# The last group's half results: evacuated by two engines, and stored from ScalarE's queue instead of SyncE's

**Chip and metric.** One core of one Trainium2 chip. The metric is the device time of one launch in microseconds (us), on the slowest (here the only) core.

## The reference

Two spectral layers and two dense layers in turn, on x of 2048 x 1024 in bf16:

```python
def _A_ref(x, w_r, w_i):                       # spectral layer
    X = rfft2(x.astype(float32)) * (w_r + 1j * w_i)
    return irfft2(X, s=(S, D)).astype(bfloat16)

def _B_ref(x, w1, b1, w2):                     # dense layer, F = 3584
    h = einsum("bsd,df->bsf", x, w1) + b1
    return einsum("bsf,fd->bsd", h * tanh(softplus(h)), w2)

for A, B in (two times the same weights):
    x = x + _A_ref(_layernorm(x), w_r, w_i)
    x = x + _B_ref(_layernorm(x), w1, b1, w2)
```

## The kernel before

The FFTs are matrix products. A spectral layer handles its frequencies in eight groups g. Step `i2` of a group gives two half results in PSUM, the memory that TensorE writes to. They are copied ("evacuated") into the tile `U` in SBUF, the on-chip memory of the tiles, in bf16. The last step, `i4`, needs `U` with other rows on the partitions, so each group is stored into DRAM (`u_scratch`) and read back transposed into `UT`. Groups 0 to 6 are stored whole; group 7, the last, is stored in two halves so that the first can leave early.

```python
def i2(g, half):
    ...                                        # matmuls into ps (lines 738 and 756)
    dst = u.ap[:, 8 * half:8 * half + 8, :].rearrange("p a b -> p (a b)")
    if g > 4 or (half == 0 and g % 2 and li):
        self.op(dve, lambda e: e.tensor_copy(dst, ps), reads=banks, parts=[u.res])            # line 764
    else:
        self.op(act, lambda e: e.activation(dst, ps, ACT.Copy), reads=banks, parts=[u.res])   # line 766

def u_turn(g, half):
    u = U[g % 3]
    if g == 7:
        h = slice(8 * half, 8 * half + 8)
        if half == 0:
            self.r_ud[g].begin()
        self.dma(sp, self.u_d[g][:, h, :], u.ap[:, h, :], f"uwh{half}", reads=[u.res], parts=[self.r_ud[g]])
    elif half:
        self.dma(sp, self.u_d[g], u.ap, f"uw{g % 3}", reads=[u.res], writes=[self.r_ud[g]])
    if g and (half == 0) == (g == 7):
        u_back(g - 1)                          # for g = 7: read-back of 6 BETWEEN the two stores
    if g == 7 and half:
        u_back(7)

def u_back(g):                                 # 16 rows x 128 x 256 bytes
    for i, prog in enumerate((sp, act) if g == 7 else (sp,)):
        l = slice(64 * i, 64 * i + 64) if g == 7 else slice(0, P)
        self.dma(prog, self.UT.ap[g:P:8, l, :], self.u_d[g][l].rearrange("l r n -> r l n"), ...,
                 reads=[self.r_ud[g]], parts=[self.UT.res])

def i4(self, lo, nb, u0, n, bank, staged=None):
    ...                                        # matmuls, line 875
    self.group(fns, reads=[self.UT.res, self.r_mt], writes=rb)    # waits for ALL of UT
    ...                                        # VectorE adds into x, line 881
```

Each engine takes its program in order: below, in evac_only, a store whose data is ready at 633.96 us is issued at 637.50, behind an older command. All DMAs (copies between DRAM and SBUF) are issued by the helper line 247, and "SPq" and "ACTq" are the sequencers of SyncE and ScalarE.

Of the kernel before, what the change touches and what calls it, by code (L numbers as in the profile page):

```python
# [179 lines left out]
class KB:  # L180
# [439 lines left out]
    def layer_A(self, li):  # L620
# [7 lines left out]
        dve, act, sp, pool = self.dve, self.act, self.sp, self.pool  # L628
# [97 lines left out]
        def i2(g, half):  # L726

            ps, banks, _ = self.pair()
            v, u = V[g % 2], U[g % 3]
            fns = []  # L730
            mov = lambda c, part: v.ap[:, 2 * c + part, :, :].rearrange("p a b -> p (a b)")

            def cls(kd, re, im):
                t = kd * 3 * P
                for dst, stats in ((re, (0, 2)), (im, (1, 0))):
                    for part in range(2):
                        c = t + stats[part] * P
                        fns.append(lambda e, dst=dst, part=part, c=c: e.matmul(  # L738
                            dst, BD[:, c:c + P], mov(kd, part), start=(part == 0), stop=(part == 1)))
            if half == 0:  # L740
                cls(0, ps[:, 0:256], ps[:, 256:512])
                cls(1, ps[:, 512:768], ps[:, 768:1024])
            else:
                cls(2, ps[:, 0:256], ps[:, 512:768])

                t = 9 * P
                if g == 0:
                    outs = [[(i, part, (0, 2)[part]) for part in range(2)] for i in range(2)]
                else:
                    outs = [[(0, 0, 0), (0, 1, 2), (1, 0, 0), (1, 1, 2)], [(0, 0, 1), (0, 1, 0), (1, 0, 2), (1, 1, 3)]]  # L750
                for m, terms in enumerate(outs):
                    for n, (i, part, tab) in enumerate(terms):
                        for kd in range(2):
                            rows = slice(64 * kd, 64 * kd + 64)
                            dst = ps[:, 512 * kd + 256 + m * P:512 * kd + 256 + (m + 1) * P]
                            fns.append(lambda e, dst=dst, rows=rows, i=i, part=part, tab=tab, n=n, last=len(terms) - 1: e.matmul(
                                dst, BD[rows, t + tab * P:t + (tab + 1) * P], v.ap[rows, 6 + part, i, :],
                                start=(n == 0), stop=(n == last)))
            self.group(fns, reads=[v.res, self.r_bd], writes=banks)
            if half == 0:  # L760
                u.res.begin()
            dst = u.ap[:, 8 * half:8 * half + 8, :].rearrange("p a b -> p (a b)")
            if g > 4 or (half == 0 and g % 2 and li):
                self.op(dve, lambda e: e.tensor_copy(dst, ps), reads=banks, parts=[u.res])  # L764
            else:
                self.op(act, lambda e: e.activation(dst, ps, ACT.Copy), reads=banks, parts=[u.res])  # L766
# [5 lines that stand above are left out]
                h = slice(8 * half, 8 * half + 8)  # L772
                if half == 0:
                    self.r_ud[g].begin()
                self.dma(sp, self.u_d[g][:, h, :], u.ap[:, h, :], f"uwh{half}", reads=[u.res], parts=[self.r_ud[g]])
            elif half:
                self.dma(sp, self.u_d[g], u.ap, f"uw{g % 3}", reads=[u.res], writes=[self.r_ud[g]])
            if g and (half == 0) == (g == 7):
                u_back(g - 1)
            if g == 7 and half:  # L780
                u_back(7)

        def u_back(g):
            for i, prog in enumerate((sp, act) if g == 7 else (sp,)):
                l = slice(64 * i, 64 * i + 64) if g == 7 else slice(0, P)
                self.dma(prog, self.UT.ap[g:P:8, l, :], self.u_d[g][l].rearrange("l r n -> r l n"), f"u{prog.name}{g % 3}",
                         reads=[self.r_ud[g]], parts=[self.UT.res])
# [10 lines left out]
        for step in range(8 + 3):  # L798
            g2, g3, g4, g5 = step, step - 1, step - 2, step - 3
            for h in range(2):  # L800
                if 0 <= g2 < 8:
                    s2(g2, h)
                if 0 <= g2 < 8 and h == 0 and li == 0:
                    filter_bins(g2)
                if 0 <= g3 < 8:
                    s3(g3, h)
                if 0 <= g4 < 8:
                    i1(g4, h)
                if 0 <= g5 < 8:
                    i2(g5, h)  # L810
                    u_turn(g5, h)
            if 0 <= g3 < 8 and g3 + 2 < 8:
                load_tabs(g3 + 2)
            if li == 0 and g2 + 2 < 8:
                load_w(g2 + 2)
            if li == 0 and 1 <= g2 < 9:
                self.keep_filter(g2 - 1)
            if li and 1 <= g2 < 5:
                load_w(g2 + 3)
            if 0 <= g4 < 8 and g4 + 2 < 8:  # L820
                load_btabs(g4 + 2)
# [275 lines left out]
```

## Time and profile before

| | before |
|---|---|
| time, 3 runs | 1071.35 us median (1070.46 to 1071.45) |
| span of the profiled run | 1068.5 us |
| TensorE busy | 973.0 us, 91% |
| TensorE's idle before line 875, for the read-backs | 27.9 us, in two waits |

The kernel is bound by TensorE. What is left to win in the spectral layers' ends is the time in which TensorE waits for `UT`; the prediction below reads that from the chain of waits, the timeline and the DMA view. One thing to know for reading them: a DMA issue's duration is the time that its *issuing engine* spends on it, not the transfer (the store of group 6 takes 0.57 us of issue and lands after 4.33 us). The transfer's end is shown as "landing", or as a DMA piece of the chain.

### The profile page before, as it was taken

The page shows a single profiled execution, that of the slowest core. Times are in us where ns is not written, and L with a number is a line of the kernel's source. Part 1 is how long each engine was busy: PE and PEld are TensorE (multiplying, and loading weights), DVE is VectorE, ACT ScalarE, POOL GpSimd, SP SyncE. Part 2 cuts the span into 40 slices and gives each one's busy share as a digit, 9 for nine tenths or more (in the row PEclk, how much of TensorE's full clock was granted, in tenths as well). Part 3 has the DMA queues.
Part 4 walks back from the last instruction along what each step waited for, and adds up shares of the span by engine and source line. Part 5 has one row for each costly group of instructions (what it writes and reads, how often), then busy time and mean ns, then how long its engine had stood idle before and what let it go on. Part 6 is the DMA issues. An engine that isn't in the chain of part 4 may idle for free. (4 is left out here: it accounts for less than half of the span.)

```text
span 1068.5 us, 14145 instructions
## 1 busy us (share of the span) xinstructions
PE 973.0 (91%) x6089; PEld 509.6 (48%) x6089; DVE 362.4 (34%) x811; ACT 330.2 (31%) x466; POOL 55.3 (5%) x86
## 2 busy tenths in 40 slices
PE   0799479999999999999969965999999999999998
PEld 0677345444444444444427744444444444444443
DVE  7887482600444200033436866451011110000111
ACT  6898253342000234300007843434300013431000
POOL 2042000000000000001310200000000000000000
PEclk9699769999999999999988985999999999999999
DMA  9678732444000122211720885144500002210000
GB/s 293 148 247 252 186 111 85 153 150 126 20 20 21 57 68 73 79 60 38 142 47 30 229 200 139 55 143 146 169 22 20 21 34 70 74 40 11 20 20 29
DMA packets 138958, 102.80 MB, mean 96 GB/s; under 512 B 59952, under 2 KB 117552, under 8 KB 138896
## 3 DMA queue, kind: packets, MB, share of 16 engines
q1 hardware_dynamic: 128528, 78.34, 25.1%
q0 software_dynamic: 7856, 22.94, 7.6%
q10 hardware_dynamic: 2512, 0.62, 0.3%
q8 instruction: 48, 0.79, 0.3%
q14 instruction: 14, 0.11, 0.0%
HBM read 80.85 MB, written 20.71 MB: 95 GB/s over the span
## 5 line engine op out<-in xcount | busy, mean ns | idle before, releaser
L930 PE MATMUL PS<-ARENA 128*128 128x512 bf16 x1792 | 393.7, 382 | 1.6 <-DVE ARENA L917 1.6
L948 PE MATMUL PS<-ARENA 128*128 128x512 bf16 x1792 | 390.0, 379 | 0.0
L934 ACT ACTIVATE ARENA<-PS,B 128x512 bf16<-128x512 f32 x224 | 153.8, 687 | 440.0 <-PE PS L930 440.0
L930 PEld LDWEIGHTS PS<-ARENA 128*128 128x128 bf16 x1792 | 175.5, 98 | 214.3 <-issue 6.0
L948 PEld LDWEIGHTS PS<-ARENA 128*128 128x128 bf16 x1792 | 174.5, 98 | 207.8
L953 DVE TENSOR_TENSOR XS<-PS,XS 128x512 bf16<-128x512 f32 x64 | 44.3, 691 | 566.1 <-PE PS L948 566.1
L436 DVE BATCH_NORM_STATS2 BN<-XS 128x6 f32<-128x512 bf16 x108 | 69.5, 673 | 7.5 <-DMA XS<-in_A_x_dram 6.3
L875 PE MATMUL PS<-MT,ARENA 128*128 128x32 bf16 (+1 forms) x768 | 24.7, 189 | 36.1 <-DMA ARENA<-u_scratch 27.9
L881 DVE TENSOR_TENSOR XS<-PS,XS 128x512 bf16<-128x512 f32 (+1 forms) x40 | 29.1, 789 | 75.8 <-PE PS L875 75.8
L575 ACT ACTIVATE ARENA<-PS 128x1024 bf16<-128x1024 f32 x16 | 16.1, 1018 | 110.8 <-PE PS L569 110.6
L875 PEld LDWEIGHTS PS<-MT,ARENA 128*128 128x128 bf16 x768 | 23.0, 101 | 39.5 <-issue 31.4
L417 ACT ACTIVATE ARENA<-XS 128x1024 bf16<-128x1024 bf16 x20 | 21.1, 1056 | 54.6 <-DVE XS L881 43.6
L695 ACT ACTIVATE ARENA<-PS 128x1024 bf16<-128x1024 f32 x32 | 33.0, 1032 | 9.0 <-PE PS L691 9.0
L650 PE MATMUL PS<-FD,ARENA 128*128 128x256 bf16 (+1 forms) x312 | 33.5, 257 | 2.4 <-DVE ARENA L577 2.4
L724 ACT ACTIVATE ARENA<-PS 128x1024 bf16<-128x1024 f32 x32 | 33.0, 1032 | 3.7 <-PE PS L717 3.7
L717 PE MATMUL PS<-ARENA 128*128 128x256 bf16 x256 | 33.2, 273 | 0.1
L699 DVE TENSOR_TENSOR ARENA<-ARENA 128x1024 bf16<-128x1024 bf16 x32 | 22.1, 690 | 28.1 <-ACT ARENA L695 22.7
L650 PEld LDWEIGHTS PS<-FD,ARENA 128*128 128x128 bf16 x312 | 26.3, 99 | 7.2 <-DVE ARENA L577 2.8
L717 PEld LDWEIGHTS PS<-ARENA 128*128 128x128 bf16 x256 | 24.6, 98 | 9.7 <-DVE ARENA L706 0.9
L912 PE MATMUL PS<-IDENT,ARENA 128*128 128x128 bf16 x256 | 21.6, 242 | 8.3 <-DVE ARENA L479 5.8
L738 PE MATMUL PS<-ARENA,BD 128*128 128x256 bf16 x192 | 25.9, 273 | 0.4 <-DVE ARENA L764 0.2
L912 PEld LDWEIGHTS PS<-IDENT,ARENA 128*128 128x128 bf16 x256 | 18.6, 109 | 14.0 <-DVE ARENA L479 6.9
(66 smaller groups left out, 517.8 us busy)
## 6 DMA issues: line engine op xcount, KB each, us to landing
ARENA<-in_B_w_dram SPq DMA_DIRECT2D x56, 512.0 KB, 4.0
ARENA<-in_B_w_dram SPq DMA_DIRECT2D x56, 256.0 KB, 4.4
u_scratch<-ARENA SPq DMA_DIRECT2D x14, 512.0 KB, 4.1
ARENA<-u_scratch SPq DMA_DIRECT2D x14, 512.0 KB, 5.3
XS<-in_A_x_dram SPq DMA_DIRECT2D x4, 1024.0 KB, 8.6
ARENA<-in_A_x_dram SPq DMA_DIRECT2D x32, 128.0 KB, 3.3
w_scratch<-ARENA POOLq DMA_DIRECT2D x8, 512.0 KB, 5.0
ARENA<-w_scratch POOLq DMA_DIRECT2D x8, 512.0 KB, 3.6
```

The source lines that it names most:

```text
L436: self.op(self.dve, lambda e: e.bn_stats(self.BN[:, j, 6 * h:6 * h + 6], self.XS[:, j, 512 * h:512 * h + 512]), reads=[self.r_xs[j]], part ...
L650: fns.append(lambda e: e.matmul(dst, at(r), FD[:, t:t + dst.shape[-1] * 2], start=start, stop=stop))
L695: self.op(act, lambda e: e.activation(x.ap.rearrange("p a b -> p (a b)"), ps, ACT.Copy, scale=SIG), reads=banks, writes=[x.res])
L717: fns.append(lambda e, c=c, part=part: e.matmul(ps[:, c * 256:(c + 1) * 256], yk.ap[:, part, c * P:(c + 1) * P], t[:, (128, 0)[part]:(384, ...
L724: self.op(act, lambda e: e.activation(v.ap[:, :, i, :], src, ACT.Copy), reads=banks, parts=[v.res])
L875: fns.append(lambda e, l=l: e.matmul(ps[:, w * l:w * l + w], self.UT.ap[:, u0 + l, :], self.MT[:, 8 * lo:8 * lo + w], start=True, stop=True))
L881: self.op(self.dve, lambda e: e.tensor_tensor(xs, src, xs, ALU.add), reads=rb, parts=self.r_xs[lo:lo + nb])
L912: fns.append(lambda e, db=db: e.transpose(PSb[:, bank, db * P:(db + 1) * P], xn.ap[:, db * P:(db + 1) * P], self.IDENT[:]))
L930: fns.append(lambda e, db=db, bank=bank, fl=fl: e.matmul(PS[:, bank, :], wb.ap[:, db, fl * P:(fl + 1) * P], x.ap[:, db, :], start=(db == 0 ...
L934: self.op(act, lambda e, bank=bank, ft=ft: e.activation(at.ap[:, ft, :], PS[:, bank, :], ACT.Mish, bias=self.B1[:, ft:ft + 1]), reads=[sel ...
L948: fns.append(lambda e, i=i, ft=ft: e.matmul(PS[:, bank, :], at.ap[:, ft, t * P:(t + 1) * P], W2[ft].ap[:, h * 512:(h + 1) * 512], start=(i ...
L953: self.op(dve, lambda e: e.tensor_tensor(xs, PS[:, bank, :], xs, ALU.add), reads=[self.r_bank[bank]], writes=[self.r_xs[j]])
```

## The change

Intent: let the last two half results be evacuated by VectorE and ScalarE side by side, and let their stores be issued by ScalarE, which is idle there, so that they don't queue behind SyncE's work.

```diff
-            if g > 4 or (half == 0 and g % 2 and li):
+            if (g > 4 and (g < 7 or half == 0)) or (half == 0 and g % 2 and li):
                 self.op(dve, ... tensor_copy ...)
             else:
                 self.op(act, ... activation Copy ...)
...
-                self.dma(sp, self.u_d[g][:, h, :], u.ap[:, h, :], f"uwh{half}", ...)
+                self.dma(act, self.u_d[g][:, h, :], u.ap[:, h, :], f"uwh{half}", ...)
```

More of the change, by code (lines that the diff above doesn't have):

```diff
@@ L774, in u_turn @@
                     self.r_ud[g].begin()
-                self.dma(sp, self.u_d[g][:, h, :], u.ap[:, h, :], f"uwh{half}", reads=[u.res], parts=[self.r_ud[g]])
+                self.dma(act, self.u_d[g][:, h, :], u.ap[:, h, :], f"uwh{half}", reads=[u.res], parts=[self.r_ud[g]])
             elif half:
```

## The prediction

> **What bounds the kernel now.** I read the page first, then the chain of waits in order of time, the timeline around the end of a spectral layer, the wait table of the DMA queue's own engine, and the DMA view in short windows. The whole kernel is bound by TensorE (973.0 of 1068.5 us busy), so a change elsewhere counts only where TensorE stands still. In section 5 of the page that is the first stage after the spectral block:
>
> ```profile
> L875 PE MATMUL PS<-MT,ARENA 128*128 128x32 bf16 (+1 forms) x768 | 24.7, 189 | 36.1 <-DMA ARENA<-u_scratch 27.9
> ```
>
> TensorE is idle for 36.1 us before this line, 27.9 of them for the bounce of U through DRAM, in two places (once a layer), 14 us each. The change can touch only these two holes. The chain of waits of the second one (start us, us, what):
>
> ```profile
> 630.11 1.24 DVE ARENA L764
> 631.36 4.33 DMA u_scratch<-ARENA
> 635.71 0.54 SPq L247
> 636.29 5.05 DMA u_scratch<-ARENA
> 641.42 4.36 DMA ARENA<-u_scratch
> 645.92 1.03 PE PS L875 x32
> ```
>
> The timeline tells which transfers these are (start us, us in issue; a DMA's line is always the helper's):
>
> ```profile
> 630.11 3.49 DVE L764 CAST ARENA<-PS 128x1024 bf16<-128x1024 f32 x3
> 631.36 0.57 SPq L247 DMA_DIRECT2D u_scratch<-ARENA  x1
> 632.03 0.54 SPq L247 DMA_DIRECT2D ARENA<-u_scratch  x1
> 632.62 2.77 SPq L247 DMA_DIRECT2D u_scratch<-ARENA  x1
> 635.71 0.54 SPq L247 DMA_DIRECT2D ARENA<-u_scratch  x1
> 636.29 1.99 SPq L247 DMA_DIRECT2D u_scratch<-ARENA  x1
> 641.41 0.54 SPq L247 DMA_DIRECT2D ARENA<-u_scratch  x1
> 641.42 0.61 ACTq L247 DMA_DIRECT2D ARENA<-u_scratch  x1
> ```
>
> By the order of the source these are: store of group 6, read-back of 5, store of group 7's first half, read-back of 6, store of 7's second half, read-back of 7 by two queues. The second half of group 7 is in SBUF at 633.60 (three casts from 630.11, 1.21 each), yet its store is issued at 636.29: SyncE's queue first spends 2.77 us issuing the first half's store, then waits until 635.71 for group 6's store to land, then issues that read-back. So 2.7 us go to the order of SyncE's queue.
>
> But the DMA engines are not idle meanwhile. The DMA view from 628 to 648 us, 0.5 us a slice:
>
> ```profile
> DMA  0006997999999999999999999200039998000027
> GB/s 16 0 0 262 385 262 151 267 289 288 264 273 418 341 285 288 231 229 282 330 289 284 223 244 303 102 0 0 0 93 279 267 273 135 2 0 0 16 59 227
> ```
>
> They are full from about 630 to 640.6, empty to 642.8 (the round trip from the last store to the first packet of the last read-back), and full again to 645.0. The only hole to be closed is 2.2 us; the bytes stay the same. In the first layer the same rows run from 114 to 131 us with a hole of 2.2 us from 125.9 to 128.1.
>
> **What the Trainium skill says.** (1) "DMA: Bandwidth & Descriptors", "Issuing engines are not separate DMA queues": transfers from any engine run on the same 16 DMA engines and interleave; a second issuing engine "will only save the time on the sequencer". So no bandwidth is to be expected, only issue order, and this case's wait is just such a case of issue order. (2) The same page, "Queues, rings and completion order": SyncE and ScalarE each own a row of rings on the same engines, "not a DMA engine or descriptor generator of their own", and an engine round-robins between rows. The trace agrees with the first half: the two halves of the last read-back are issued 0.01 us apart, but from 643.2 to 643.6 us SyncE's queue moves 440 packets and ScalarE's 7, and from 644.0 to 644.4 it is 11 and 435. One command is served after the other, they do not alternate. (3) "PSUM — Partial Sum Buffer", "Engine vs sequencer instructions": ScalarE's queue is strict FIFO. A DMA issue that waits on ScalarE therefore holds up the evacuation behind it; the trace before has no such place. (4) "TensorE: Matmul & The Clock Gate", "What's actually happening": after an idle window of about 3.4 us the clock halves and a free-running window decides when it returns. The trace agrees on the fall: the granted clock is 0.50 from 636 us and until 651. A hole of 12 instead of 14 us still falls that low, so no clock is gained; the phase of its return may move by a microsecond or so.
>
> **The change part by part.** *Evacuation of the last half.* Before: DVE, 1.21 us, ends 633.60. After: ScalarE, 1.03 us (same shape, line 766: 1023 to 1165 ns, median 1032). But the first half's store now stands ahead of it in ScalarE's queue and waits for DVE's cast of that half, which ends at 632.44 (630.11 + 1.24, then 1.21 started at 631.23). With an issue of 0.61 us (the issue that ScalarE has here) the activation starts at 633.1 and ends at 634.1. Using two engines thus gains nothing: it is 0.5 us later than DVE was, because ScalarE first waits for DVE. ScalarE itself is idle from 629.9 to 641.4, and VectorE loses a cast that nobody waits behind; neither matters.
>
> *First store.* SyncE no longer stands 2.77 us in its issue, but gains nothing either: its next command, the read-back of 6, waits for group 6's store to land at 635.7 as before.
>
> *Second store.* If ScalarE's issues go through without being held, it is issued at 634.1 + 0.05, or 2.1 us earlier than 636.29, and, more to the point, ahead of the read-back of 6 (635.71, 512 KB in 256-byte packets, some 2 us of packets). In the order of commands it now follows the first half directly. Its landing: first half at 638.6 as before (632.62 + 6.0), plus 256 KB at the measured 280 GB/s, 0.9 us: 639.5, against 641.34. The read-back of 6 is pushed behind by that much, but still ends with the full stretch at 640.6.
>
> *Last read-back.* Issued at 639.5; 1.35 us later its first packet (641.41 to 642.75 before) at 640.9; 2.2 us of packets to 643.1; landing 0.75 after the last packet as before (645.0 to 645.78): 643.8. Against 645.78 that is **2.0 us**. If the stores overtake more of the backlog, by the round robin of the two rows, the hole closes wholly: 2.2, and with some better packing at most 2.7. It cannot be much more, since the same 2.6 MB or so stand ahead of the end either way.
>
> *Downstream.* The matmuls of line 875, their additions and the statistics start as soon as U is there and move forward as a block: the first matmul follows the landing by 0.14 us. The weight loads that follow on SyncE wait for the same landing and are not needed before 663 us. So both layers' gain reaches the end: 2 × 2.0 to 2 × 2.4 = 4.0 to 4.8 us, or 1066.6 to 1067.4 from the median 1071.35.
>
> **The rivals.** *R1: ScalarE is held in issue as SyncE was.* The 2.77 us of the first store show that a command issued into a backlog can hold its engine. If that limit belongs to the shared generator and not to SyncE's own queue, ScalarE stands from 632.5 to 635.4, activates to 636.4, issues the second store at 636.5 behind the read-back of 6, is held again for some 1.8 us, and everything ends as before: gain 0, perhaps 0.2 us lost, **1071.3**. For it: the strictly serial service of the two halves above. Against it: in that same pair ScalarE's issue took 0.61 us while SyncE's command was being served, so it wasn't held there; but only one command was ahead then, where now there would be two or three. I can't decide this from the trace, and give it about a third.
>
> *R2: the transfer is hidden anyway by the backlog.* The stores land earlier, but the read-back of 6 comes later by the same amount and the last read-back queues behind it on SyncE's half. Bytes are conserved, so the end isn't delayed beyond 643.8 unless the stores slow group 6's store, which the read-back of 6 waits for. Should they delay it by 0.9 us, the gain falls to some 1 us a layer: 1069. One chance in ten.
>
> *R3: contention or the clock costs more than the order gains.* Two rows active at once interleave 256-byte reads and 2 KB writes, and TensorE's clock returns later by the phase of its window. At half clock until 651 and again from 656 to 669 us in the second layer, a shift of 1 to 2 us is possible: up to 1072.5. Below one in ten.
>
> *R4: the first store goes at once, not behind the backlog.* Then it lands by 636 and the second by 638; the hole closes fully and the queues overlap: 1066, included in the main case.
>
> **Range and chances.** The main case with R4 has some 0.57 (1066 to 1067.4), R2 0.1 (1069), R1 with R3 0.33 (1071 to 1072). The weighted mean is 0.57 × 1066.7 + 0.1 × 1069 + 0.33 × 1071.4 = 1068.5; I take a value nearer the likelier heap, 1067.6. The runs before spread over 1.0 us, so the range is 1064.9 to 1071.8. Two per cent are 21 us; both holes together have 28 us, of which the change reaches at most 6, so within 2% is nearly certain.
>
> **What would show each step.** Right: in the timeline, two stores on ScalarE's queue near 632.5 and 634.1 us (layer-relative), each with an issue under 1 us; the activation at line 766 between them; the read-back of 6 on SyncE still near 635.7; the last read-backs issued before 640; the empty DMA slices gone; TensorE's idle before line 875 at 23 to 24 us from the DMA instead of 27.9. R1: an issue of over 2 us on ScalarE, and the last read-back still near 641.4. R2: the last store lands early, but the read-back of 6 or of 7 lands later after its issue than 5.2 and 4.4 us. R3: TensorE's idle falls, but the time doesn't; then the granted clock after line 875 is to be looked at. What would make the prediction wrong as a whole: a store that finishes far ahead of the backlog while the read-backs run above 280 GB/s, or a read-back on SyncE that is held by ScalarE's stores.

## The result

The changed kernel ran in 1067.28 us (median of 4, 1066.74 to 1067.37), against 1070.9 us for the kernel before on the same chip (4 runs, 1069.44 to 1071.45). The ratio is 0.9967, with a 95% interval of 0.995 to 0.9985. Ratios here are the mean time of one kernel's fast runs over that of the other's in the same rounds, so they are not quite the ratio of the medians. It is 3.6 us, or 0.3%; the interval excludes 1.

The group of line 875 on the page of the changed kernel (columns: busy us, mean ns | idle us of the engine before it, and what ended most of it):

```profile
L875 PE MATMUL PS<-MT,ARENA 128*128 128x32 bf16 (+1 forms) x768 | 24.6, 188 | 32.1 <-DMA ARENA<-u_scratch 23.9
```

27.9 us of waiting became 23.9: 2.0 us in each layer (13.99 to 11.97 and 13.88 to 11.88). The chain of waits of the second layer, changed kernel:

```profile
631.95 1.03 ACT ARENA L766
633.00 5.10 DMA u_scratch<-ARENA
638.18 4.68 DMA ARENA<-u_scratch
642.99 1.03 PE PS L875 x32
```

Before there were three transfers in this chain, and an issue of SyncE between two of them. Now there are two: the second store and the last read-back. The read-back of 6 is gone from it. The timeline of the changed kernel, second layer (start us, us in issue or execution). In this profile everything in this place stands 0.93 us earlier than in the one of before (line 764's run starts at 626.70 instead of 627.63), so add 0.93 to compare:

```profile
626.70 4.84 DVE L764 CAST ARENA<-PS 128x1024 bf16<-128x1024 f32 x4
630.43 0.60 SPq L247 DMA_DIRECT2D u_scratch<-ARENA  x1
631.12 0.54 SPq L247 DMA_DIRECT2D ARENA<-u_scratch  x1
631.57 0.33 ACTq L247 DMA_DIRECT2D u_scratch<-ARENA  x1
631.95 1.02 ACT L766 ACTIVATE ARENA<-PS 128x1024 bf16<-128x1024 f32 x1 [3.00 <-DVE ARENA L764]
633.00 0.33 ACTq L247 DMA_DIRECT2D u_scratch<-ARENA  x1
635.09 0.54 SPq L247 DMA_DIRECT2D ARENA<-u_scratch  x1
638.16 0.53 SPq L247 DMA_DIRECT2D ARENA<-u_scratch  x1
638.18 0.62 ACTq L247 DMA_DIRECT2D ARENA<-u_scratch  x1
```

Both stores leave ScalarE in 0.33 us each, into the same backlog (transfers issued and not yet moved) in which SyncE's took 2.77 and 1.99 us. The second store is issued 2.1 us before SyncE's read-back of 6 (635.09) and no longer after it. And the activation shows the price of the order inside ScalarE's queue: "3.00 <-DVE": ScalarE waited for VectorE before it could start.

The DMA view of the changed kernel from 627.1 to 647.1 us (0.5 us a slice, so that it lines up with the one of before):

```profile
DMA  0007997999999999999999994999930000389999
GB/s 0 0 0 311 336 262 159 280 291 281 260 277 428 326 292 328 347 303 334 382 302 289 274 182 76 259 281 247 192 58 1 0 0 12 95 230 341 347 337 293
```

The hole before the last read-back, three empty slices between two that are partly filled, has shrunk to one slice at four tenths. The work now ends some 2 us sooner.

### The profile page after: what moved, and what is told of

Read it like the earlier page. It is cut to its first block, busy times and chain, and to the rows that moved or that the text cites. A ratio compares the mean times of both kernels' runs of the same rounds, so it can differ in the third digit from the quotient of the medians.

```text
span 1065.6 us, 14051 instructions
## 1 busy us (share of the span) xinstructions
PE 967.1 (91%) x5995; PEld 510.3 (48%) x6089; DVE 360.9 (34%) x809; ACT 332.6 (31%) x468; POOL 55.4 (5%) x86
## 5 line engine op out<-in xcount | busy, mean ns | idle before, releaser
L930 PE MATMUL PS<-ARENA 128*128 128x512 bf16 x1752 | 388.2, 381 | 4.4 <-DVE ARENA L917 2.4
L948 PE MATMUL PS<-ARENA 128*128 128x512 bf16 x1754 | 387.4, 379 | 2.0
L875 PE MATMUL PS<-MT,ARENA 128*128 128x32 bf16 (+1 forms) x768 | 24.6, 188 | 32.1 <-DMA ARENA<-u_scratch 23.9
L717 PEld LDWEIGHTS PS<-ARENA 128*128 128x128 bf16 x256 | 24.7, 98 | 9.7 <-DVE ARENA L706 0.9
```

The source lines that it names most:

```text
L717: fns.append(lambda e, c=c, part=part: e.matmul(ps[:, c * 256:(c + 1) * 256], yk.ap[:, part, c * P:(c + 1) * P], t[:, (128, 0)[part]:(384, ...
L875: fns.append(lambda e, l=l: e.matmul(ps[:, w * l:w * l + w], self.UT.ap[:, u0 + l, :], self.MT[:, 8 * lo:8 * lo + w], start=True, stop=True))
L930: fns.append(lambda e, db=db, bank=bank, fl=fl: e.matmul(PS[:, bank, :], wb.ap[:, db, fl * P:(fl + 1) * P], x.ap[:, db, :], start=(db == 0 ...
L948: fns.append(lambda e, i=i, ft=ft: e.matmul(PS[:, bank, :], at.ap[:, ft, t * P:(t + 1) * P], W2[ft].ap[:, h * 512:(h + 1) * 512], start=(i ...
```

## The experiments

Two calls of four kernels, five timed rounds each, with the kernel before on the same chip. All eight give correct results.

My theory was the **order theory**: the gain comes from the second store no longer standing behind the read-back of 6 in SyncE's order, and the DMA engines' own backlog sets how much it can be. Its rivals: the **two-engines theory** (the evacuation is what helps) and the **second-queue theory** (what counts is that the stores have a queue of their own, which isn't held in issue).

The waits table of each kernel has a line for TensorE's wait for the read-backs (us in total, times, longest). In the order before, queue_only, evac_only, order_only, second_store_act:

```profile
PE PS L875 <- DMA ARENA<-u_scratch: 27.9, 2, 14.0
```

```profile
PE PS L875 <- DMA ARENA<-u_scratch: 23.8, 2, 12.0
```

```profile
PE PS L875 <- DMA ARENA<-u_scratch: 28.0, 2, 14.0
```

```profile
PE PS L875 <- DMA ARENA<-u_scratch: 24.7, 2, 12.6
```

```profile
PE PS L875 <- DMA ARENA<-u_scratch: 24.5, 2, 12.3
```

**queue_only: the stores alone move.**

```diff
 # against the kernel before
-                self.dma(sp, self.u_d[g][:, h, :], ...)
+                self.dma(act, self.u_d[g][:, h, :], ...)
```

> Only the stores move to ScalarE's queue; both halves stay with VectorE's cast. Order theory (the gain comes from the second store no longer standing behind the read-back of group 6 on SyncE's queue): the whole gain of 3.6 us stays, perhaps 0.3 us more, since the second half is ready at 633.6 instead of 633.9 us; 1066.8 to 1067.5. Two-engines theory (the gain comes from the evacuation): none of it, 1070.9. TensorE's idle before the first matmul after U: 23.2 to 24.0 us in sum by the order theory, 27.9 by the other.

Measured: 1067.55 us (1067.06 to 1067.88), ratio 0.9969 (0.9956 to 0.9981), wait 23.8 us. That is the whole gain, without a second engine for the evacuation. The extra 0.3 us that I thought possible isn't seen; it would be below the resolution of these runs.

**evac_only: the evacuation alone moves.**

```diff
 # against the kernel before
-            if g > 4 or (half == 0 and g % 2 and li):
+            if (g > 4 and (g < 7 or half == 0)) or (half == 0 and g % 2 and li):
```

> Only the evacuation of the second half moves to ScalarE; both stores stay on SyncE's queue. Order theory: no gain, 1070.5 to 1071.3, because the second store is issued at 636.3 us whatever the evacuation does, and the data is there at 633.1 instead of 633.6 us. Two-engines theory: the gain of 3.6 us or a good part of it, 1067.3 to 1069.

Measured: 1071.22 us (1069.98 to 1071.62), ratio 1.0001 (0.9987 to 1.0014), wait 28.0 us. The two-engines theory falls. The timeline of this kernel, second layer:

```profile
632.94 1.02 ACT L766 ACTIVATE ARENA<-PS 128x1024 bf16<-128x1024 f32 x1 [2.21 <-PE PS L756]
633.50 3.16 SPq L247 DMA_DIRECT2D u_scratch<-ARENA  x1
636.91 0.54 SPq L247 DMA_DIRECT2D ARENA<-u_scratch  x1
637.50 1.87 SPq L247 DMA_DIRECT2D u_scratch<-ARENA  x1
```

Here the two engines really do work side by side (ScalarE waits for TensorE, not for VectorE), and the second half is in SBUF at 633.96 us. SyncE issues its store at 637.50. The 3.5 us between are the first store's issue, the wait for group 6's store, and the read-back of 6: a half result that is ready sooner only waits longer.

**order_only: no engine and no queue changes; SyncE issues the second store ahead of the read-back of 6.**

```diff
 # against the kernel before
-            if g and (half == 0) == (g == 7):
+            if g and half:
                 u_back(g - 1)
```

> No engine and no queue changes: SyncE merely issues the second store of group 7 before the read-back of group 6. Order theory: most of the gain; the first store's issue still holds SyncE until 635.4 us, the second goes out at once after it (some 0.9 us earlier than before and ahead of 512 KB), lands near 639.3 instead of 641.3, and the last read-back is issued 2 us earlier: 1066.9 to 1068. Second-queue theory (what counts is that ScalarE's queue isn't held and its stores pass the backlog on SyncE's rings): less than half of the gain, 1069.5 to 1071.

Measured: 1067.99 us (1066.75 to 1068.78), ratio 0.9974 (0.9961 to 0.9986), wait 24.7 us. Of the 4.0 us of TensorE's wait that the change removes, the order alone removes 3.2. On the clock of the kernel before (line 764's run starts 0.62 us earlier here) the second store is issued at 635.45 instead of 636.29 and lands at 639.2 instead of 641.3. Timeline, second layer:

```profile
632.00 2.78 SPq L247 DMA_DIRECT2D u_scratch<-ARENA  x1
634.83 0.43 SPq L247 DMA_DIRECT2D u_scratch<-ARENA  x1
635.30 0.54 SPq L247 DMA_DIRECT2D ARENA<-u_scratch  x1
638.68 0.54 SPq L247 DMA_DIRECT2D ARENA<-u_scratch  x1
638.69 0.61 ACTq L247 DMA_DIRECT2D ARENA<-u_scratch  x1
```

SyncE is still held for 2.78 us by the first store, and that costs only the difference between 24.7 and 23.9 us, 0.4 us a layer. So by these waits, of one profile each, the second-queue theory explains about a fifth of the gain; the order explains the rest. The times agree, but are too scattered to tell order_only from queue_only.

**second_store_act: the first store goes back to SyncE, so that ScalarE doesn't wait for VectorE.**

```diff
 # against the changed kernel
-                self.dma(act, self.u_d[g][:, h, :], ...)
+                self.dma(act if half else sp, self.u_d[g][:, h, :], ...)
```

> As the changed kernel, but the first store goes back to SyncE, so that ScalarE's activation no longer waits for VectorE's cast: it starts at 632.0 and ends at 633.1 us instead of 633.9, and the second store is issued 0.9 us earlier than in the changed kernel. Conserved-bytes theory: nothing more than 0.3 us a layer is won, because the DMA engines are full until the last read-back's first packet: 1066.6 to 1067.4. If instead the landing of the second store follows its issue one for one, 0.9 us a layer: 1065.5.

Measured: 1068.26 us (1066.95 to 1069.52), ratio 0.9976 (0.9963 to 0.9988), wait 24.5 us. The point estimate lies outside what I expected for the conserved-bytes theory; it is not better than the changed kernel but, by the wait, 0.3 us a layer worse. Timeline, second layer:

```profile
630.56 1.02 ACT L766 ACTIVATE ARENA<-PS 128x1024 bf16<-128x1024 f32 x1 [2.21 <-PE PS L756]
631.08 3.23 SPq L247 DMA_DIRECT2D u_scratch<-ARENA  x1
631.67 0.33 ACTq L247 DMA_DIRECT2D u_scratch<-ARENA  x1
637.89 4.67 DMA ARENA<-u_scratch
```

(The last line is from the chain of waits.) The second store is issued 0.7 us earlier than in the changed kernel, once both are put on one clock (this kernel's line 764 runs 0.60 us before the changed one's), and lands 5.5 us later. But now the *first* store sits in SyncE's backlog, and lands 6.8 us after its issue at 631.08; the last read-back waits for both. What was won on one store was lost on the other. These lines also settle the rival R1 of the prediction: from 631.08 to 634.31 SyncE is held in its issue, and in the middle of that ScalarE's issue takes 0.33 us. So the hold is not in something that both queues share; it goes with SyncE's queue, which had the backlog. Whether ScalarE would be held with as much queued on its own side was not tried.

**changed_again** and **extra_readback: what sets the end after the change?** The second reads group 6 once more, 512 KB in packets of 256 bytes, into a place that nobody uses.

```diff
 # extra_readback, against the changed kernel
             if g and (half == 0) == (g == 7):
                 u_back(g - 1)
+            if g == 7 and half == 0:
+                extra = self.alloc("EXTRA", 0, [P, P])
+                self.dma(sp, extra.ap[6:P:8, :, :], self.u_d[6].rearrange("l r n -> r l n"), "uextra",
+                         reads=[self.r_ud[6]], writes=[extra.res])
```

> The changed kernel as it is, for comparison on the same chip as the next three: 1066.7 to 1067.8, ratio to before near 0.9967; the stores on ScalarE's queue at the same two places of its order, TensorE's idle for the read-backs 23.9 us in sum.

> The changed kernel with 512 KB more of 256-byte packets: right behind the read-back of group 6 SyncE reads group 6 once more into a free place that nobody uses (result unchanged). Conserved-bytes theory (after the change the DMA engines' throughput sets the end, no longer the order): the last read-back's packets come later by 512 KB at some 285 GB/s, 1.8 us a layer, so 3.2 to 3.8 us in all: about 1070.5 to 1071. If the end is set by latencies and order (the second store's landing), the extra packets go beside them: at most 1 us in all, 1067.3 to 1068.3.

Measured: changed_again 1066.85 us (1066.65 to 1067.8), ratio 0.9966 (0.9954 to 0.9979), so the result repeats; extra_readback 1071.7 us (1071.27 to 1072.43), ratio 1.0011 (0.9997 to 1.0024). The added bytes cost 4.85 us between the medians, and 4.8 us of TensorE's wait (23.9 to 28.7). They are fully on the path: after the change nothing is left beside which 512 KB could hide. The whole delay comes after the last read-back's issue, which stands 11.48 us after the start of line 764's run in both kernels; from there it takes 7.23 us instead of 4.68 (chain of waits, second layer):

```profile
640.05 7.23 DMA ARENA<-u_scratch
```

The extra read stands ahead of half of the last read-back on SyncE's own queue, so this run alone doesn't part the engines' throughput from the order of that queue. But the other half, on ScalarE's queue, is late too: it lands 6.4 us after its issue instead of 4.7.

That the added bytes cost more than the 3.2 to 3.8 us that I expected fits the rate. The DMA view of extra_readback from 640 to 647 us (0.175 us a slice):

```profile
GB/s 290 266 252 215 193 208 222 211 209 205 206 206 200 205 205 206 205 206 205 203 202 206 203 209 219 215 220 215 206 206 206 202 195 151 101 64 40 16 0 0
```

It runs at some 205 GB/s, not at the 285 that I had taken from the stretch before, and 512 KB at 205 GB/s are 2.6 us against the 2.4 us a layer that were measured. The DMA engines are not idle in that stretch: a packet of 256 bytes takes longer, 26 ns from 640.8 to 642.4 us against 18 ns from 639.4 to 640.2 (the packets' time divided by their number). The changed kernel's last read-back ends in the same way, at 195 GB/s from 641.0 to 641.6 us. Why a packet takes longer there I did not find out.

**halves** and **quarters: let `i4` start on the part of the last read-back that is there.** `i4` works in four groups of 32 columns; each now waits only for its own piece of group 7.

```diff
 # quarters, against the changed kernel, shortened (halves: two pieces of 64)
+        self.UTq = [Res(f"UTq{i}") for i in range(4)]
         def u_back(g):                          # g < 7: as before, and marks all of UTq
+            for i in range(4):
+                prog, l = (sp, act)[i % 2], slice(32 * i, 32 * i + 32)
+                self.dma(prog, self.UT.ap[g:P:8, l, :], self.u_d[g][l].rearrange("l r n -> r l n"), f"uq{i}",
+                         reads=[self.r_ud[g]], parts=[self.UT.res, self.UTq[i]])
...
-        self.group(fns, reads=[self.UT.res, self.r_mt], writes=rb)
+        t = self.group(fns, reads=[self.UTq[u0 // 32], self.r_mt], writes=rb)
+        self.UT.res.r(self.pe, t)
```

> The changed kernel in which the first two of the four groups of line 875 wait only for the first half of the last read-back. In the profile of before and after that half (SyncE's) lands 0.8 to 0.9 us ahead of ScalarE's, because the two commands are served one after the other. If so, TensorE starts 0.8 us earlier in each layer and VectorE's chain of four additions (4.6 us) covers the second half: 1.6 us in all, 1065.4 to 1066. If the two halves were served alternately, nothing: 1067.3.

> As halves, with the last read-back in four pieces on the two queues in turn, each with its own wait. By serial service the first piece lands 3 quarters of 2.2 us, 1.6 us, before the last; VectorE's additions (1.2 us each) hide the others: 3 us in all, 1064 to 1064.8. Against it: two more issues of 0.54 to 0.6 us each, and a latency of 2.1 us outside the packets that doesn't shrink. If issue or latency eats it: no better than halves.

Measured: halves 1064.87 us (1063.03 to 1065.75), ratio 0.9944 (0.9932 to 0.9957); quarters 1063.84 us (1063.26 to 1065.56), ratio 0.9938 (0.9926 to 0.9951). Against changed_again on the same chip that is 2.0 and 3.0 us by the medians, where I expected 1.6 and 3. TensorE's wait for the read-backs fell from 23.9 to 22.0 and 20.6 us. Neither kernel's runs overlap the changed kernel's. The chain of waits of quarters, second layer:

```profile
630.69 5.16 DMA u_scratch<-ARENA
635.91 3.14 DMA ARENA<-u_scratch
639.19 1.03 PE PS L880 x32
640.24 4.63 DVE XS L887 x4
```

The store is what it was in the changed kernel (5.10 us), and the read-back that TensorE waits for went from 4.68 to 3.14 us. VectorE's four additions then run without a gap (4.63 us as before), so the later pieces are hidden behind them. This is the best of the versions tried; whether quarters beat halves is within the scatter of the two.

## Why the prediction was right

Predicted 1067.6 us, measured 1067.28, and the main case's sum was 4.0 to 4.8 us where 3.6 (ratio and medians) to 4.2 (second chip) were measured. That 1067.6 lies within 0.4 us of the result is partly luck: it was the main case shifted towards rivals that did not come, and it started from 1071.35 us. From 1070.9 the main case alone gives 1066.1 to 1066.9, a little too much gain. Point by point:

- **The place.** The gain is in the waits before line 875: 27.9 to 23.9 us, within the 23 to 24 foretold. Downstream moved as a block: the second layer's first matmul of line 875 starts 2.93 us earlier in the profile and the span ends 2.9 us earlier. (In that profile the sum is 2.9 and not 4.0, because the changed kernel's profiled run was 1.05 us late at group 6's store of the first layer, ahead of every changed instruction.)
- **Two engines gain nothing.** Right. evac_only shows it (1.0001), and the changed kernel's activation waits 3.00 us for VectorE. Its size was a little off: I took ScalarE's issue at 0.61 us, from its read-back; the stores took 0.33. The second store is issued at 633.9 (on the clock of before), not 634.15.
- **The second store ahead of the read-back of 6.** Right, and order_only shows that this is where the gain lies. Its landing: 639.5 foretold, 633.00 + 5.10 + 0.93 = 639.0 measured. The stores overtook a little of the backlog, though less than R4 had it: the first, foretold for 638.6 (636 by R4), landed at 637.6 (631.57 + 5.1 + 0.93).
- **The last read-back.** Issue 639.5 foretold, 639.1 measured; landing 643.8 foretold, 638.18 + 4.68 + 0.93 = 643.8 measured. Two errors cancel: the issue came 0.4 us earlier, and the last read-back took 4.7 instead of the 4.4 us of before, while the read-back of 6 was still being moved. That the landing fits to 0.1 us is luck.
- **R1, ScalarE held in issue** (a third of the chances) did not happen: 0.33 us. second_store_act shows both queues at the same moment, 3.23 us on one and 0.33 on the other. The pair of read-backs that I had read as evidence for R1 tells of the order of service, not of the issue.
- **R2, the backlog gives part of it back,** is there in small: group 6's store lands 4.6 us after its issue instead of 4.3, and so the read-back of 6 is issued 0.3 us later (635.09 + 0.93 against 635.71). By R2's own sign, the read-backs of 6 and 7 land 5.6 and 4.7 us after their issue instead of 5.2 and 4.4. It did not eat the gain.
- **R3, contention or the clock,** did not happen: the wait fell by 4.0 us and the time by 3.6 to 4.2. The clock did not behave as foretold, though: in the changed kernel's profile it was 1.00 again from 647 us (648 on the clock of before), where before it was 0.50 until 651. No gain from that shows, as the first matmul and the end of the span moved by the same 2.9 us.
- **The bound by bytes.** The prediction took the hole of 2.2 us as the likely cap; 2.0 was reached. In finer slices the hole is only 1.9 us (640.8 to 642.7), so the cap was read a little too wide. extra_readback shows that added bytes are now paid in full. But the fixed rate of 280 GB/s in that sum does not hold to the end: the last read-back falls to 195 GB/s in the changed kernel and runs at 205 in extra_readback.

## What to carry to other kernels

Look in an in-order queue for a transfer whose data is ready while an older command waits for something else, and ask first whether the *order* can be mended: one line's move on SyncE took away four fifths of the wait that the whole change took away. Cap the hoped-for gain by the idle slices of the DMA engines and not by the queue's wait (about 2 us of hole here, where the queue's order alone wasted 2.7). And when the bytes have become the bound, let the consumer start on the first piece: that gave another 2 to 3 us.

## What the Trainium skill lacked or had wrong

- "DMA: Bandwidth & Descriptors", "Issuing engines are not separate DMA queues", says that a second issuing engine saves only the sequencer's issue time, usually small relative to the DMA. Here that time was 2.77 and 1.99 us for stores of 256 KB that land in 5 to 6 us, and the order behind it cost more (order_only: 3.2 of the 4.0 us of wait). The page's first statement agrees with the runs: no bandwidth was gained. The same 3.67 MB of the second layer's end took 13.5 us without the hole before (629.7 to 645.1) and 13.4 us in the changed kernel (628.8 to 642.1).
- "Perfetto Trace Analysis", "DMA Instruction — HWDGE (DVE, Sync)", lists the steps of an issue, a wait for the lock of a shared descriptor generator among them. It gives no time for an issue into a backlog, and doesn't say that the hold can be on one issuing queue alone: 3.23 us on SyncE, and within them 0.33 us on ScalarE (second_store_act).
- "DMA: Bandwidth & Descriptors", "Queues, rings and completion order", says that an engine alternates between rows at packet granularity, with at most 64 descriptors in a packet. Two read-back halves issued 0.01 us apart on two rows were served almost wholly one after the other (440 packets to 7, then 11 to 435), and halves and quarters make use of it. This does not show the page wrong, nor does the prediction's "they do not alternate": a half is 1024 rows of 256 bytes, 64 for each of 16 engines if they are spread evenly (an estimate), which would fit in one packet of the page's largest size. No run shows where the packets end. The stores of the changed kernel did mix with the read-backs: from 634.8 to 635.2 us SyncE's queue moved 200 packets and ScalarE's 43. Which of the two happens when is open.
- No page gives a measured trn2 rate for read-backs of 256-byte rows to 16 partitions ("DMA: Bandwidth & Descriptors" has only an overhead of each small packet): some 285 GB/s in the middle of the stretch, 205 in extra_readback.
